# Attention over a pooled memory and experts on one core: sums as eight products, a maximum in pieces, another opening and smaller transfers

## The chip, the cores and the metric

The kernel runs on one core of one Trainium2 chip. The metric is the device time of one execution in microseconds, the median of several runs. The profile is one execution taken by the hardware profiler; its times are counted from the first instruction. PE is the tensor engine, DVE the vector engine, ACT the scalar engine, POOL GpSimd, SP the engine that issues nearly all transfers.

## The reference

There are 8 batches with 8 heads, 576 tokens and 64 values per head; phi holds 32 memory slots per head. Then comes a mixture of 8 experts (512 to 1024 to 512) over all 4608 tokens.

```python
a = np.exp(phi - np.max(phi, axis=2, keepdims=True))        # over the tokens
a = a / (np.sum(a, axis=2, keepdims=True) + 1e-09)
k_m = np.einsum('bhsm,bhsd->bhmd', a, k)
v_m = np.einsum('bhsm,bhsd->bhmd', a, v)
scores = np.matmul(q, k_m.transpose(0, 1, 3, 2)) / np.sqrt(64)
attn = softmax(scores)                                      # over the 32 slots
x = np.matmul(attn, v_m)                                    # heads joined: 512 per token
e_idx = argmax(x @ w_gate + modality_bias[modality_id])     # one expert per token
out = gate_w * (np.maximum(x @ w1[e_idx], 0) @ w2[e_idx])
```

## The kernel before, in words

**Layout.** The eight heads are two groups (NG) of four (HG): the groups lie on the two halves of the 128 partitions, 64 places of 9 tokens each. The memory of a batch is built first. `mem_max` (L309) takes the maximum of phi, by a `fold` (L291) of four DVE operations; `first_max` (L301) does it for batch 0 with reductions. `mem_exp` (L350) forms the exponentials, `mem_sums` (L374) adds them up on POOL, or on DVE for batch 0. `kv_products` (L392) multiplies them with keys and values in tiles of 64 x 32 (L403), and then adds over the partitions by one product of the sums with `sides` (L408), a matrix of ones and zeros that parts the two groups. `first_products`, `first_sums`, `first_divide`, `first_even`, `first_odd` (L410 to L477) are the steps of batch 0.

**Attention.** `q_turn` (L536) turns q in place on DVE. `scores` and `first_scores` (L541, L556) multiply; `soften` (L582) turns the scores to tokens, takes the maximum, subtracts it and has ACT form the exponential; `normalise` (L603) divides by the sum plus EPS and turns back. For batch 0's first part of four places, `first_weights` (L627) and `first_split` (L644) do it group by group. `a_split` (L652) splits the weights into a rounded upper half (ACT) and a remainder (DVE), in tiles xa (first part) and xb (second part), and for odd batches stores both to DRAM, where only a fallback reads them.

**Experts.** The expert that the bias alone prefers is guessed early (`guess`, L215) and its w1 and w2 are loaded; `verdict` at the end says whether a token chose another one, and only then does the fallback `any_experts` run. `value_products` (L724) multiply the pooled values with w1, so that `hidden` (L765) needs one product of attention weights with that matrix vw, in three terms (upper x upper, remainder x upper, upper x remainder). `relu` (L786) evicts on ACT (hh) and DVE (hl). `outputs` (L805) multiplies with w2 in three terms; `store` (L832) scales by the gate on ACT and issues the store on SP.

**The order.** All instructions are issued in an order that a planner works out before the build (`weave`, L1131): two lists, attention and experts, each with costs per engine (`TAKES`, L860), places in the progress of the expert work (`due`) and earliest times (`floor`). `weave` follows both lists and takes the next attention step when its due progress is reached and its inputs would be ready. An output product counts fully in the progress, a hidden one 0.35 (`WORTH`, L881). `HOLD` (L1138) says how much attention work may be queued on DVE in front of the eviction of the next hidden product. `AHEAD` and `EARLIER` (L1116) shift the memory steps of a batch: at L1123 the value of EARLIER is subtracted, so that {3: -4.0} puts batch 3 four units later. The opening, batch 0, is a list written out by hand in `plan_first` (L914).

**Idle products.** `warm_small` (L162) issues small products of zeros (64 x 32, 16 columns), `warm` (L156) large ones (128 x 128, 512 columns). `BUSY` (L79) has the counts before the opening; `nothing(n)` in `plan_first` (L945, L947, L989) puts n large ones between its steps.

**Transfers.** SP's queue has, in the opening: phi of batch 0, k, v, the first part of q; then, once the expert is guessed, w1 in two halves, modality ids and w_gate between them, w2, the rest of q, phi of batch 1 (L223 to L239); then k and v of batch 1 and q of batch 1 in 32 pieces (`more_keys`, L489). k and v of a batch are one transfer each (`load_kv`, L177).

## Time and profile before

| | |
|---|---|
| median of 3 runs | 389.59 us (389.57 to 389.6) |
| profiled execution | 389.69 us, of which 387.9 us is the span from first to last instruction |
| DVE, ACT, POOL busy | 244.7, 141.3, 45.8 us |
| mean granted clock of PE | 0.994 |
| moved by DMA | 56.89 MB, mean 147 GB/s |

The page lists busy times of the engines, the span in 40 slices, the DMA queues, the chain that ended last and the costliest groups of instructions. In a row of a timeline stand the start, the length, the engine with the line of the kernel, the operation, what it writes and reads, and the count of instructions that were merged; in square brackets is the idle time of the engine just before, and what ended it. A product of f32 operands shows as two records.

### The profile page before, as it was taken

To read this page: it belongs to the slowest core of one execution; us is meant where nothing else is said; L and a number is where in the kernel's file an instruction comes from. 1 tells how busy PE (TensorE), PEld (TensorE's weight loads), DVE (VectorE), ACT (ScalarE), POOL (GpSimd) and SP (SyncE) were. 2 spreads that over 40 slices of the span, in tenths; PEclk is the share of its full clock that TensorE was granted. 3 is DMA by queue.
4 is the path that set the end of the run, shared out by engine and by line. 5 is a ranking of instruction groups with operands and counts; after the bars stand their busy time and mean duration, and the time that the engine had idled before them with its cause. 6 is when DMAs were issued, how large, how long until landed. Compare 5 with 4: busy or idle time off the path is not lost.

```text
span 387.9 us, 9645 instructions
## 1 busy us (share of the span) xinstructions
PE 375.3 (97%) x3891; PEld 303.3 (78%) x3893; DVE 244.7 (63%) x613; ACT 141.3 (36%) x327; POOL 45.8 (12%) x116
## 2 busy tenths in 40 slices
PE   6899999999999999999999999999999999999993
PEld 3577976889779886788879887798868878698982
DVE  4787756895786389836786476864887467750400
ACT  2382524425234243433433334323443325241410
POOL 4347030023000400030000300003000200000000
PEclk9999999999999999999999999999999999999997
DMA  8998679875761397639712397614411011531111
GB/s 300 379 394 183 103 140 344 225 210 150 243 120 42 94 298 184 208 82 276 119 34 56 75 300 126 255 28 119 182 29 42 15 30 27 198 102 32 28 36 55
DMA packets 91307, 56.89 MB, mean 147 GB/s; under 512 B 69236, under 2 KB 74356, under 8 KB 91252
## 3 DMA queue, kind: packets, MB, share of 16 engines
q1 hardware_dynamic: 90976, 55.87, 51.4%
q8 instruction: 33, 0.54, 0.6%
q10 hardware_dynamic: 276, 0.30, 0.2%
q14 instruction: 22, 0.18, 0.2%
HBM read 37.28 MB, written 18.87 MB: 145 GB/s over the span
## 4 chain that ended last, share of the span: by engine, by line
PE 85%; DVE 4%; SPq 4%; DMA 3%; ACT 1%; issue 1%; ACTq 0%
PE pe L816 47%; PE pe L779 24%; PE pair L403 4%; PE pe L732 3%; DMA q_sb<-in_q_dram 3%; SPq L195 3%; PE pair L548 2%; PE pair L679 1%; SPq L178 1%; DVE vwl L154 1%; PE pair L148 1%; PE pair L732 1%; PE pair L408 1%; DVE xbl L662 0%; ACT ob L829 0%
## 5 line engine op out<-in xcount | busy, mean ns | idle before, releaser
L816 PE MATMUL pe<-w2h,hh 128*128 128x512 f32 x288 | 116.3, 404 | 0.0
L816 PE MATMUL pe<-w2h,hl 128*128 128x512 f32 x288 | 112.4, 390 | 0.0
L816 PE MATMUL pe<-w2l,hh 128*128 128x512 f32 x288 | 110.3, 391 | 0.0
L796 DVE SCALAR_TENSOR_TENSOR hl<-pe,hh 128x256 fp32r<-128x256 f32 (+2 forms) x158 | 58.3, 392 | 43.1 <-ACT hh L792 42.3
L816 PEld LDWEIGHTS pe<-w2h,hh 128*128 128x128 f32 x288 | 54.1, 188 | 19.8 <-issue 9.7
L792 ACT ACTIVATE hh<-pe 128x256 fp32r<-128x256 f32 (+2 forms) x158 | 53.4, 362 | 41.6 <-PE pe L779 41.2
L816 PEld LDWEIGHTS pe<-w2l,hh 128*128 128x128 f32 x288 | 54.0, 188 | 11.8
L816 PEld LDWEIGHTS pe<-w2h,hl 128*128 128x128 f32 x288 | 54.2, 188 | 9.6
L829 ACT ACTIVATE ob<-pe,gates 128x512 f32<-128x512 f32 x36 | 24.6, 687 | 73.4 <-PE pe L816 48.1
L779 PE MATMUL pe<-xbh,vwh 128*128 128x320 f32 x128 | 40.3, 315 | 0.1
L779 PE MATMUL pe<-xbh,vwl 128*128 128x320 f32 x128 | 39.6, 309 | 0.0
L779 PE MATMUL pe<-xbl,vwh 128*128 128x320 f32 x128 | 39.6, 309 | 0.0
L779 PE MATMUL pe<-xah,vwh 128*128 128x256 f32 x124 | 35.2, 287 | 1.5 <-DVE hl L796 0.7
L779 PE MATMUL pe<-xal,vwh 128*128 128x256 f32 x124 | 35.0, 284 | 0.3 <-DVE xal L662 0.3
L779 PE MATMUL pe<-xah,vwl 128*128 128x256 f32 x124 | 34.9, 283 | 0.0
L337 POOL COPY ts<-tm 32x4 f32<-32x4 f32 x24 | 4.8, 199 | 198.8 <-DVE tm L329 198.1
L779 PEld LDWEIGHTS pe<-xah,vwh 128*128 128x128 f32 x124 | 23.6, 191 | 4.2 <-ACT xah L648 1.6
L779 PEld LDWEIGHTS pe<-xbh,vwh 128*128 128x128 f32 x128 | 24.0, 188 | 1.7 <-issue 0.9
L779 PEld LDWEIGHTS pe<-xbl,vwh 128*128 128x128 f32 x128 | 24.1, 188 | 0.3
L779 PEld LDWEIGHTS pe<-xal,vwh 128*128 128x128 f32 x124 | 23.7, 191 | 0.8 <-DVE xal L662 0.5
L779 PEld LDWEIGHTS pe<-xbh,vwl 128*128 128x128 f32 x128 | 24.0, 188 | 0.0
L779 PEld LDWEIGHTS pe<-xah,vwl 128*128 128x128 f32 x124 | 23.7, 191 | 0.0
(173 smaller groups left out, 430.0 us busy)
## 6 DMA issues: line engine op xcount, KB each, us to landing
kv_sb<-in_k_dram SPq DMA_DIRECT2D x8, 1152.0 KB, 7.2
kv_sb<-in_v_dram SPq DMA_DIRECT2D x8, 1152.0 KB, 9.7
out_dram<-ob SPq DMA_DIRECT2D x64, 128.0 KB, 2.4
q_sb<-in_q_dram SPq DMA_DIRECT2D x112, 72.0 KB, 2.8
ph<-in_phi_dram SPq DMA_DIRECT2D x7, 576.0 KB, 4.3
raw<-in_moe_w_dram SPq DMA_DIRECT2D x2, 1024.0 KB, 6.4
raw<-in_moe_w_dram SPq DMA_DIRECT2D x1, 1280.0 KB, 10.2
out_dram<-ob SPq DMA_DIRECT2D x4, 256.0 KB, 2.1
```

The costliest lines, as they stand in the source:

```text
L148: nc.tensor.transpose(dst, src, ident[:rows, :rows])
L154: nc.vector.tensor_tensor(l, src, h.bitcast(F32), op=ALU.subtract)
L195: nc.sync.dma_start(*later.pop(0))
L337: nc.gpsimd.tensor_copy(ts_[BL * a:BL * (a + 1)], live["tm"][BL * o:BL * (o + 1)])
L403: nc.tensor.matmul(live["kvp"][M * j:M * (j + 1), g], lhsT=pe[half, j, c * M:(c + 1) * M], rhs=kv_sb[half, :, j, c * D:(c + 1) * D], start ...
L548: nc.tensor.matmul(sc[g][M * j:M * (j + 1), a, 0:QC * BL], lhsT=kvT[b][rows, 0, M * j:M * (j + 1)], rhs=qT[rows, j, a], start=True, stop=T ...
L732: nc.tensor.matmul(pvs[g][M * j:M * (j + 1), :], lhsT=vT[b][rows, j, :], rhs=raw1[rows, j, cols], start=True, stop=not more, tile_position ...
L779: nc.tensor.matmul(ph[:, 0:n], lhsT=(vl if k == 2 else vh)[:, g, cols], rhs=xl if k == 1 else xh, start=(g == k == 0), stop=(g == NG - 1 a ...
L792: nc.scalar.activation(hs[0][:, f, h0:h0 + p1 - p0], live["ph", f][:, p0:p1], AF.Relu)
L796: nc.vector.scalar_tensor_tensor(hl, live["ph", f][:, p0:p1], 0.0, hh.bitcast(F32), op0=ALU.max, op1=ALU.subtract)
L816: nc.tensor.matmul(po, lhsT=tile_columns(hl if n == 1 else hh, f, t), rhs=(w2l if n == 2 else w2h)[:, f, :], start=(f == n == 0), stop=(f ...
L829: nc.scalar.activation(ob, po, AF.Copy, scale=gate_of(b, t))
```

## The change

- **Idle products**: 97 small and 3 large ones ahead of the opening in place of 92 and 10; the 1, 4 and 3 large ones between its steps go.
- **Sums**: in `kv_products` the product with `sides` becomes eight products of 64 x 32 with a column of ones, one per head; `sides` and its fills go.
- **Maximum**: for batch 1 the fold goes; reductions take the maximum of heads 0 and 1 before the second scores of batch 0, of head 2 before batch 0's second normalisation, of head 3 before the remainder of its split.
- **EPS**: batch 0's first part keeps its weights in a tile with a 33rd column that holds EPS, so that the sum contains it and the addition goes.
- **Order of the opening**: `first_odd` for the keys stands ahead of the turns of q, `first_even` for the values ahead of `first_keys`; floors move by 0.5 to 1.
- **Planner**: `EARLIER` {3: -4.0} becomes {7: -6.0}; `HOLD` rises from 1.9, 2.4, 2.2 to 2.2, 3.0, 2.7; the cost of the key and value products falls from 2.6 to 2.5, and kinds "m1" (DVE 0.55) and "m2" (DVE 1.1) are added in `TAKES`.
- **Transfers**: w1 in four pieces of 256 columns; k and v of batches 1 to 7 in two pieces each, by columns; the stored operands with runs of one place (NG x 128 values) instead of all places of a partition. The fallback reads them accordingly.
- **Last tile**: the last store of the last batch is scaled half by ACT, half by DVE, and the halves are stored by the queues of SP and ACT.

```diff
@@ -76,7 +76,7 @@
     EPS = 1e-9
-    BUSY = 92, 10
+    BUSY = 97, 3
...
@@ -135,8 +134,8 @@
-    xa_dram = [[dram.tile([P, NG * RA * P], F32R, name=f"xa_dram{p}{x}") for x in "hl"] for p in range(NPAIR)]
-    xb_dram = [[dram.tile([P, NG * RB * P], F32R, name=f"xb_dram{p}{x}") for x in "hl"] for p in range(NPAIR)]
+    xa_dram = [[dram.tile([RA, P, NG * P], F32R, name=f"xa_dram{p}{x}") for x in "hl"] for p in range(NPAIR)]
+    xb_dram = [[dram.tile([RB, P, NG * P], F32R, name=f"xb_dram{p}{x}") for x in "hl"] for p in range(NPAIR)]
@@ -168,6 +167,9 @@
+    def flat(x, n):
+        return x.rearrange("p i g c x -> p (i g c x)").rearrange("p (n y) -> p n y", n=n)
+
@@ -175,7 +177,11 @@
-        nc.sync.dma_start(kv_sb[:, t], halves((k, v)[t], b))
+        src = halves((k, v)[t], b)
+        pieces = 2 if b else 1
+        for i in range(pieces):
+            cols = slice(i * (QC * D // pieces), (i + 1) * (QC * D // pieces))
+            nc.sync.dma_start(kv_sb[:, t, :, cols], src[:, :, cols])
@@ -219,8 +225,9 @@
         for hf in range(2):
-            cols = slice(hf * 512, (hf + 1) * 512)
-            nc.sync.dma_start(raw1[:, :, cols], first[:, :, cols])
+            for c0 in (2 * hf, 2 * hf + 1):
+                cols = slice(c0 * 256, (c0 + 1) * 256)
+                nc.sync.dma_start(raw1[:, :, cols], first[:, :, cols])
@@ -298,13 +305,16 @@
+    def heads_max(b, js):
+
+        if js.start == 0:
+            live["top", b] = wk.tile([P, HG, M], F32, name="top")
+        src = phs[b].rearrange("p j (c m) -> p j m c", m=M)
+        nc.vector.tensor_reduce(live["top", b][:, js], src[:, js], axis=AX.X, op=ALU.max)
+
     def first_max():
-
-        top = wk.tile([P, HG, M], F32, name="top")
-        src = phs[0].rearrange("p j (c m) -> p j m c", m=M)
         for js in (slice(0, HG // 2), slice(HG // 2, HG)):
-            nc.vector.tensor_reduce(top[:, js], src[:, js], axis=AX.X, op=ALU.max)
-        live["top", 0] = top
+            heads_max(0, js)
@@ -394,7 +404,7 @@
-        live["psum"] = pk[:, 0, 2 * D:2 * D + NG]
+        live["psum"] = pk[:, :, 2 * D]
@@ -405,7 +415,13 @@
-        nc.tensor.matmul(live["psum"], lhsT=sums.rearrange("p j m -> p (j m)"), rhs=sides, start=True, stop=True)
+        for j in range(HG):
+            for g in range(NG):
+                half = slice(QP * g, QP * (g + 1))
+                nc.tensor.matmul(
+                    pk[M * j:M * (j + 1), g, 2 * D:2 * D + 1], lhsT=sums[half, j], rhs=ones_c[half],
+                    start=True, stop=True, tile_position=(QP * g, M * j),
+                )
@@ -583,7 +599,9 @@
         if step in (None, 0) and groups in (None, 0):
-            live["a", b, part] = by_token(wk.tile([P, 2 * NG * RB * M], F32, name="a", bufs=2), n, M)
+            live["a", b, part] = live["a0"][:, :, :, :, 0:M] if b == part == 0 else by_token(
+                wk.tile([P, 2 * NG * RB * M], F32, name="a", bufs=2), n, M
+            )
@@ -591,7 +609,7 @@
-                        a[:, g].rearrange("p a c m -> p a (c m)"), sc[g][:, :, RA * part * BL:(RA * part + n) * BL]
+                        a[:, g] if b == part == 0 else a[:, g].rearrange("p a c m -> p a (c m)"), sc[g][:, :, RA * part * BL:(RA * part + n) * BL]
@@ -631,8 +649,8 @@
             sa, ra = (wk.tile([P, 2 * NG * RB], F32, name=y, bufs=2)[:, 0:n] for y in ("sa", "ra"))
-            nc.vector.tensor_reduce(sa, x, axis=AX.X, op=ALU.add)
-            nc.vector.tensor_scalar_add(sa, sa, EPS)
+            whole = live["a0"][:, g].rearrange("p a c m -> p (a c) m")
+            nc.vector.tensor_reduce(sa, whole, axis=AX.X, op=ALU.add)
@@ -663,7 +681,7 @@
-                nc.sync.dma_start(d.bitcast(F32), x.rearrange("p i g c x -> p (i g c x)").bitcast(F32))
+                nc.sync.dma_start(d.bitcast(F32).rearrange("n p x -> p n x"), flat(x, n).bitcast(F32))
@@ -831,6 +849,15 @@
         def finish(po):
+            if b == B - 1 and t is None:
+                rows = out[S * (b - 1):S * (b + 1)].rearrange("(p c) d -> c p d", c=QC)[QC - 1]
+                first, second = slice(0, DM // 2), slice(DM // 2, DM)
+                obs = [wk.tile([P, DM], F32, name="ob", bufs=2)[:, 0:DM // 2] for _ in range(2)]
+                nc.scalar.activation(obs[0], po[:, first], AF.Copy, scale=gate_of(b, t))
+                nc.vector.tensor_scalar(obs[1], po[:, second], gate_of(b, t), None, op0=ALU.mult)
+                nc.sync.dma_start(rows[:, first], obs[0])
+                nc.scalar.dma_start(rows[:, second], obs[1])
+                return
...
@@ -895,7 +922,7 @@
         for name, after, what, late in (
-            ("max", [], mem_max, 0.0),
+            *((("max", [], mem_max, 0.0),) if b > 1 else ()),
@@ -942,20 +969,18 @@
         add(("guess",), "guess", [], guess)
-        nothing(1)
         add(("exp", 0), "first exp", [("top", 0)], mem_exp, 0)
-        nothing(4)
...
         add(("kn", 0), "kn0", [("k", 0), ("sums", 0)], first_divide)
+        add(("ko", 0), "ko0", [("kn", 0)], first_odd, 0)
         turns(0, 0, 9.5)
-        add(("ko", 0), "ko0", [("kn", 0)], first_odd, 0)
...
         add(("v", 0), "v0", [("exp", 0)], first_products, 1)
+        add(("vn", 0), "vn0", [("v", 0)], first_even, 1)
         add(("kT", 0), "kT", [("ko", 0)], first_keys)
-        add(("vn", 0), "vn0", [("v", 0)], first_even, 1)
@@ -986,7 +1011,6 @@
-        nothing(3, "pe")
@@ -994,10 +1018,11 @@
         some_hidden("he", "h0y", [("x", 0, 0)], range(1, 3), range(1, 2))
-        add(("start",), "start", [], lambda: None, floor=25.0)
-        turns(1, 0, 26.5)
-        turns(1, 1, 27.2)
-        add(("s", 0, 1), "s1", [("qt", 0, 1, 1), ("vwl", 0, 1)], first_scores, RA, RB, floor=28.6)
+        add(("start",), "start", [], lambda: None, floor=24.0)
+        turns(1, 0, 25.5)
+        turns(1, 1, 26.2)
+        add(("max", 1, 0), "m2", [], heads_max, 1, slice(0, 2), floor=26.5)
+        add(("s", 0, 1), "s1", [("qt", 0, 1, 1), ("vwl", 0, 1)], first_scores, RA, RB, floor=27.6)
@@ -1049,6 +1074,11 @@
                 add(("bias", pair + 1), "nothing", [], biases, pair + 1)
+        if b == 0:
+            names = [x[0] for x in todo]
+            for j, before in ((3, ("x", 0, 1)), (2, ("n", 0, 1, 0))):
+                todo.insert(names.index(before), (("max", 1, j - 1), "m1", [], heads_max, (1, slice(j, j + 1))))
+            todo += [(("max", 1), "nothing", [("max", 1, 2)], lambda: None, ())]
@@ -1086,7 +1116,7 @@
-            stage(experts, ("w2", c), "w2", [], first_w2, c, floor=21.0 + 0.7 * c)
+            stage(experts, ("w2", c), "w2", [], first_w2, c, floor=20.5 + 0.7 * c)
@@ -1113,7 +1143,7 @@
-    AHEAD, EARLIER, SPREAD = (5.8, 5.0), {3: -4.0}, 0.55
+    AHEAD, EARLIER, SPREAD = (5.8, 5.0), {7: -6.0}, 0.55
@@ -1135,7 +1165,7 @@
-        HOLD = {"h0": 1.9, "h1": 2.4, "h3": 2.2}
+        HOLD = {"h0": 2.2, "h1": 3.0, "h3": 2.7}
@@ -1211,13 +1241,12 @@
         warm(BUSY[1])
+        live["a0"] = wk.tile([P, NG, 2, RA, M + 1], F32, name="a0")
+        nc.gpsimd.memset(live["a0"][:, :, :, :, M:M + 1], EPS)
...
         nc.scalar.activation(minus, ident, AF.Copy, scale=-1.0)
-        for g in range(NG):
-            for e in range(NG):
-                nc.gpsimd.memset(sides[QP * g:QP * (g + 1), e:e + 1], float(g == e))
...
```

More of the change, by code (lines that the diff above doesn't have):

```diff
@@ L103, in attn_moe @@
     places = const.tile([P, 2], F32, name="places")
-    sides = const.tile([P, NG], F32, name="sides")
     busy = const.tile([P, 512], BF16, name="busy")
@@ L864, in attn_moe @@
         "exp": (0.0, "T1.5 A0.7"), "exp0": (0.35, "D1.5 A0.7"), "first exp": (0.35, "D1.5 A0.7"), "first sums": (0.0, "T1.9"), "sums": (0.0, "P2.9"),
-        "vwp": (1.15, ""), "vwpu": (1.25, "A1.1"), "vwu": (0.0, "A1.15"), "vwl": (0.0, "D1.35"),
[1 row of a table removed]
[2 rows of a table added]
         "kT": (0.45, "A0.4"), "vT": (0.3, "A0.35"), "kvT": (0.45, "A0.4"),
@@ L1309, in any_experts @@
                 for x, d in zip(xa + live["xb"], xa_dram[pair] + xb_dram[pair]):
-                    nc.gpsimd.dma_start(x.rearrange("p i g c x -> p (i g c x)"), d)
+                    n = d.shape[0]
+                    nc.gpsimd.dma_start(flat(x, n), d.rearrange("n p x -> p n x"))
                 for i in range(2):
```

3 rows, old and new, of the table TAKES are left out of this document.

## The prediction

> **What bounds the kernel now.** I read the page first, then the waits of TensorE (PE), then the timeline of the first 45 us engine by engine, then the chain that ended last, then the tail.
>
> ```profile
> span 387.9 us, 9645 instructions
> PE 375.3 (97%) x3891; PEld 303.3 (78%) x3893; DVE 244.7 (63%) x613; ACT 141.3 (36%) x327; POOL 45.8 (12%) x116
> ```
>
> PE is busy for 97% of the span, and no other engine comes near. So the kernel is a stream of matrix products with a start, a few holes and a tail, and an edit can only win by shortening a product, closing a hole, or shortening start or tail. The holes of PE, by what ended them (total, times, longest):
>
> ```profile
> PE pair L148 <- DVE top L306: 1.1, 1, 1.1
> PE pe L779 <- DVE hl L796: 0.7, 1, 0.7
> PE pair L566 <- ACT kT L518: 0.5, 1, 0.5
> PE pe L779 <- ACT xah L659: 0.5, 1, 0.5
> PE pair L732 <- ACT kvT L523: 0.4, 1, 0.4
> PE pe L779 <- DVE xal L662: 0.3, 1, 0.3
> PE pair L148 <- DVE keys L466: 0.3, 1, 0.3
> PE pe L779 <- ACT xah L648: 0.3, 1, 0.3
> ```
>
> No DMA stands in this list, and nearly all of it lies in the opening; only the lines of L796, L659 and L662, 1.5 us together, lie behind it. The opening on PE, from the second of the large idle products on (start, length, engine and line):
>
> ```profile
> 3.12 0.63 PE L159 MATMUL pair<-busy 128*128 128x512 bf16 x1 [0.22 <-issue]
> ...
> 6.77 0.30 PE L148 MATMUL pair<-ident,top 128*128 128x128 f32 x1 [1.05 <-DVE top L306]
> 6.91 0.38 PE L159 MATMUL pair<-busy 128*128 128x512 bf16 x1
> 7.46 0.44 PE L361 MATMUL pe<-ident,topc 128*64 128x128 f32 x4 [0.17 <-DVE peak L212]
> 7.83 1.04 PE L159 MATMUL pair<-busy 128*128 128x512 bf16 x4
> 8.97 0.36 PE L251 MATMUL pair<-row,ones_r 1*128 1x17 f32 x2
> 9.26 2.19 PE L422 MATMUL pair<-kv_sb,exp 64*64 64x128 f32 x72
> 11.51 0.29 PE L433 MATMUL pair<-ones_c,sums 64*64 64x1 f32 x8
> 11.65 2.17 PE L422 MATMUL pe<-kv_sb,exp 64*64 64x128 f32 x72
> 14.15 0.43 PE L148 MATMUL pair<-ident,keys 128*128 128x128 f32 x2 [0.32 <-DVE keys L466]
> 15.04 1.07 PE L566 MATMUL pair<-q_sb,kT 32*32 32x128 f32 x64 [0.46 <-ACT kT L518]
> ```
>
> This is one chain through four engines: maximum, exponentials, products with keys (9.26) and values (11.65), the turned keys (14.15), the scores (15.04). After the scores DVE works off a softmax for two head groups, and PE last waits for the second of them:
>
> ```profile
> 22.02 0.82 PE L159 MATMUL pe<-busy 128*128 128x512 bf16 x2
> 23.09 0.38 PE L779 MATMUL pe<-xah,vwh 128*128 128x256 f32 x1 [0.26 <-ACT xah L648]
> ```
>
> From 23.09 us on PE runs dense. Whatever the opening saves counts if it moves this point; what it saves elsewhere does not.
>
> **The idle products.** Seven large ones go ahead of 6.77, where PE stands idle for 1.05 us waiting for DVE: worth nothing by themselves. The single one (6.91) is followed by a wait for DVE: nothing. The four (7.83) stand ahead of the key products, which could start up to 0.2 us sooner (9.26 less the end of the row vector's product, without the queue in front); but the products for the sums at 11.51 wait for DVE's sums, so the values start where they did: nothing. The last ones (22.02) stand in front of a wait and hide nothing but it: nothing. What they did besides is keep PE occupied; if that was needed, the price is the first rival's. Five more small ones are a few hundredths ahead of an idle PE.
>
> **Keys before the turns of q.**
>
> ```profile
> 12.74 0.71 DVE L539 STREAM_TRANSPOSE q_sb<-q_sb 128x512 f32<-128x512 f32 x1 [0.31 <-DMA q_sb<-in_q_dram]
> 13.38 0.82 DVE L466 SCALAR_TENSOR_TENSOR keys<-pair,recs,even 128x64 f32<-128x64 f32 x4
> ```
>
> The keys sat behind the first turn, which sat behind q's transfer; they now start up to 0.64 us sooner (13.38 - 12.74). But PE can turn them only after the value products (11.65 + 2.17 = 13.82), so at most 0.33 us before 14.15; ScalarE (ACT) now copies the even value halves ahead of the turned keys; and the scores need both turns of q, which end where they did, since DVE does the same three pieces in another order. Bounds 0 and 0.33; I take 0.1, near the lower end, because the second turn ends late either way.
>
> **The column of EPS.**
>
> ```profile
> 18.65 0.17 DVE L635 TENSOR_SCALAR sa<-sa 128x8 f32<-128x8 f32 x1
> ```
>
> ```profile
> 22.64 0.41 ACT L648 CAST xah<-aT 128x256 fp32r<-128x256 f32 x1 [0.44 <-DVE aT L642]
> ```
>
> Each head group loses one such addition, and both lie on DVE's chain towards the second copy at 22.64: 2 x 0.17 = 0.34 us. The sums read 33 elements in place of 32, about 0.01 us each; strided rows cost something between nothing and a tenth of six operations of this size (0.25). I take 0.35 for the additions and nothing for the stride. With the 0.1 above, the copy ends at 22.6 in place of 23.05, and the dense stream starts **0.45 us earlier** (bounds 0.1 and 0.7). The next thing late could be the weights:
>
> ```profile
> 9.10 0.39 SPq L223 DMA_DIRECT2D raw<-in_moe_w_dram  x1
> ```
>
> ```profile
> raw<-in_moe_w_dram SPq DMA_DIRECT2D x2, 1024.0 KB, 6.4
> ```
>
> The first half of w1 is on chip at about 9.10 + 6.4 = 15.5, and is read only after the scores (15.04 + 1.07). In quarters the same bytes move, with two more issues on SP's queue at 0.39 each ahead of w2, the rest of q and phi of batch 1; that is 0.8 us on loads that are limited by bytes. Nothing to 0.3 us; I take nothing. Later keys, values and the stored operands in smaller pieces make SP issue about 14 more transfers of half the size; no wait of PE names a DMA, so nothing, within 0.3 either way.
>
> **The maximum of batch 1 in pieces.** The fold of four operations leaves DVE's queue; four reductions of one head each come in, two alone and two together. The two together stand behind the later turns of q and in front of the softmax that waits for the second scores:
>
> ```profile
> 31.15 0.91 DVE L593 STREAM_TRANSPOSE a<-pair 128x320 f32<-128x320 f32 x2 [1.85 <-PE pair L566]
> ```
>
> DVE idles 1.85 us there, enough for two heads (the opening's own maximum of four heads ends the 1.05 us hole, so a head is below that). The other two stand in front of operations that wait for ACT. Cover exists, so nothing; should phi of batch 1 be late, everything behind on DVE is, by up to 1 us.
>
> **Eight products for the sums**, in batches 1 to 7 (chain that ended last: start, length, count):
>
> ```profile
> 171.66 2.18 PE pair L403 x144
> 173.84 0.31 PE pair L408 x2
> ```
>
> ```profile
> 192.10 0.19 PE pair L528 x8
> ```
>
> One product goes (two records, 0.31 us); eight small ones come (sixteen records). At the rate of the key and value products, 2.18/144 = 15 ns, they take 0.24; at that of L528, 0.19/8 = 24 ns with the switch of shape in it, 0.38. So between +0.07 and -0.07 per batch. I take 0.21 x 0.15 = 0.03 of gain, since they continue the pattern of the products before them, times seven: **0.2 us** (bounds -0.5 and 0.5).
>
> **The order planned anew.** Batch 3's memory steps move earlier by 4 of the planner's units, batch 7's later by 6, and attention work may queue on DVE up to 0.3 to 0.6 us deeper ahead of evictions (HOLD).
>
> ```profile
> 163.06 0.39 PE L779 MATMUL pe<-xah,vwh 128*128 128x256 f32 x1 [0.74 <-DVE hl L796]
> ```
>
> This hole is DVE's backlog: batch 3's gate, and right behind it the maximum of batch 4, all in front of the evictions of batch 3's hidden part. With batch 3 earlier, the gate is out of the way. Of the 0.74 I take 0.7. The two holes of batch 1 (0.5 and 0.3 in the list) lie on its own softmax, for which no due time changes; only its maximum has gone from the queue. Of 0.8 I take 0.2. For batch 7:
>
> ```profile
> 332.63 0.68 DVE L662 TENSOR_TENSOR xal<-aT,xah 128x512 fp32r<-128x512 f32 x1
> ```
>
> ```profile
> 341.06 5.75 PE pe L779 x48
> ```
>
> Its operands are ready 7.7 us before PE reads them; 6 units, about 6 us of output products, fit, barely. Sum **0.9 us** (bounds -1 and 1.5).
>
> **The last tile** is scaled by ACT and DVE, half each, and stored by two queues:
>
> ```profile
> 381.54 0.69 ACT L829 ACTIVATE ob<-pe,gates 128x512 f32<-128x512 f32 x1 [4.75 <-PE pe L816]
> ```
>
> Half a row on ACT took 0.41 (the copy at 22.64), so 0.28 less, and half the bytes per transfer: **0.3 us** (0.1 to 0.4). Nothing queues behind either.
>
> **Sum.** 0.45 + 0.2 + 0.9 + 0.3 = 1.85 us from the profiled execution's 389.69: 387.84. That execution stands 0.1 above the median of 389.59, so 387.7.
>
> **Rivals.**
> *The clock.* The first large product took 0.63 us, the one at 6.91 only 0.38: PE ran at half clock at first and at full clock once it had been occupied. At the end it falls back (third-last number: granted clock):
>
> ```profile
> 383.00:383.50 0.50, 0.00 (x0) 0.00 (x0) 0.00 (x0) 0.00 (x0) 0.00 (x0) 0.93 0.78 283
> 383.50:384.00 0.50, 0.00 (x0) 0.00 (x0) 0.00 (x0) 0.00 (x0) 0.00 (x0) 0.50 0.60 209
> ```
>
> The last product was out before 381.54, so about 2 us of idleness were enough. In the new opening the three large products are over by 3.12 + 2 x 0.63 = 4.4, and only short products come until 9.26. If the key products then run at half clock, they take 2.2 us more; the values end at 16.0, the keys turn 1.85 later, and with 0.45 back the opening loses 1.4: 389.69 + 1.4 - 1.4 (the other three terms) - 0.1 = **389.6**, no change. Against it: the pause contains real products, and I can't see what the clock counts. Chance 0.2. The Trainium skill, "TensorE: Matmul & The Clock Gate", section "The HAM clock gate", says that the full clock is granted after about 3.4 us of sustained activity and withdrawn after an idle window of that length. By it the shortened warm-up would be too short and the streams would lose half of one window, an estimate of 1.7 us, so about 389.1; the trace's withdrawal after some 2 us is sooner than its rule.
> *The clock through both streams*, keys and values: 2.19 + 2.17 lost, 0.33 + 0.45 saved, so 3.6; 389.59 + 3.6 - 1.4 = **391.8**, slower. It decides as soon as more than the key products run slow. Chance 0.07.
> *DVE's deeper queue.* A hole as at 163.06 may open in each hidden part of batches 2 to 7, twelve places, because the planner lets attention work in ahead of evictions. At 0.4 us in half of them, 2.4, without the 0.9 of the replanning: 389.59 - 0.95 + 2.4 = **391.0**, slower. It decides once a backlog outlasts the four banks that PE may fill ahead. For it: the one such hole is there already. Against it: evictions idle between pieces in all other places. Chance 0.15.
>
> **Numbers.** Forecast 0.58, clock low for the keys 0.2, for both 0.07, deeper queue 0.15. A measurement here can tell 0.2%, 0.8 us. The forecast's own range is 386.6 to 388.8; the range given reaches over the first rival to 390.3. Of these four, in this order, faster: 0.56 + 0.05 + 0 + 0.01 = 0.62; same: 0.02 + 0.14 + 0 + 0.05 = 0.21; slower: 0 + 0.01 + 0.07 + 0.09 = 0.17.
>
> **What would show it.** Right: the second group's first hidden product near 22.6; one hole fewer behind 100 us; a last ACT step of about 0.4; the sums' segment below 0.31. Wrong: key products of over 3 us, new waits of L779 on hl, or a product that waits for a transfer.

## The result, and the profile after

The changed kernel takes **391.7 us** in the median of 7 runs (390.52 to 393.31), the kernel before 389.6 us (389.35 to 390.19, 7 runs) on the same chip: a ratio of 1.0058, interval 1.0035 to 1.0081. It is slower by about 0.6%, 2.1 us, where 1.9 us of gain had been forecast. Two executions far above all others (418.53 us of the kernel before, 738.26 us of e15 below) count in no ratio. The profiled execution took 392.31 us, its span 390.5 against 387.9.

The page of the changed kernel first: PE is still the bound, busy for as long as before (375.3 us then), in a span that is 2.6 us longer. Since fifteen large idle products went and PE is busy for as long without them, other products must have become longer.

```profile
span 390.5 us, 9854 instructions
PE 375.7 (96%) x3981; PEld 303.7 (78%) x3981; DVE 245.1 (63%) x611; ACT 140.6 (36%) x327; POOL 45.5 (12%) x113
```

PE's waits in the changed kernel (total, times, longest):

```profile
PE pair L147 <- POOL mine L213: 3.4, 1, 3.4
PE pair L438 <- ACT exp L381: 0.6, 1, 0.6
PE pe L797 <- ACT xah L666: 0.6, 1, 0.6
PE pair L544 <- DVE a L611: 0.6, 1, 0.6
```

The wait ahead of the first turned maximum (L147, then L148) was 1.1 us and is 3.4, mostly because the seven large idle products that filled it are gone; the maximum also comes 0.45 us later (7.22 against 6.77). All three holes behind 60 us (0.5, 0.3 and 0.7 us) are gone; one of 0.6 at L544 is new. The timeline of the opening on PE shows where the rest is:

```profile
7.22 0.45 PE L147 MATMUL pair<-ident,top 128*128 128x128 f32 x1 [3.42 <-POOL mine L213]
8.05 0.70 PE L371 MATMUL pe<-ident,topc 128*64 128x128 f32 x4 [0.38 <-DVE peak L218]
8.75 0.57 PE L258 MATMUL pair<-row,ones_r 1*128 1x17 f32 x2
9.95 4.12 PE L438 MATMUL pair<-kv_sb,exp 64*64 64x128 f32 x72 [0.63 <-ACT exp L381]
13.84 0.34 PE L449 MATMUL pair<-ones_c,sums 64*64 64x1 f32 x8
14.02 3.09 PE L438 MATMUL pe<-kv_sb,exp 64*64 64x128 f32 x72
17.05 0.44 PE L147 MATMUL pair<-ident,keys 128*128 128x128 f32 x2
18.01 1.07 PE L582 MATMUL pair<-q_sb,kT 32*32 32x128 f32 x64 [0.53 <-ACT kT L534]
...
25.84 0.39 PE L797 MATMUL pe<-xah,vwh 128*128 128x256 f32 x1 [0.62 <-ACT xah L666]
```

Put beside the opening shown in the prediction: the key products start 0.69 us later (9.95 against 9.26) and last 4.12 us for the same 72 products (2.19); the values last 3.09 (2.17). The same instructions on the same operands in nearly twice the time: PE's clock was low, through the keys and into the values. The page's row of the granted clock doesn't show it, because it has no record ahead of the first rise; that rise stands in the trace's clock records at 15.93 us, and at 4.55 us in the kernel before. The scores start at 18.01, 2.97 us late, and the second group's first hidden product at 25.84, 2.75 late. From scores to that product it is 7.83 us, 8.05 before.

From there the stream to the last product's start takes 383.25 - 25.84 = 357.41 us; before, 381.06 - 23.09 = 357.97. So all parts of the change that act in the stream brought 0.56 us together. The last tile, in the timeline of the end:

```profile
383.25 0.39 PE L834 MATMUL pe<-w2l,hh 128*128 128x512 f32 x1
383.72 0.47 ACT L856 ACTIVATE ob<-pe,gates 128x256 f32<-128x256 f32 x1 [4.75 <-PE pe L834]
384.22 0.36 SPq L858 DMA_DIRECT2D out_dram<-ob  x1
384.23 0.48 DVE L857 TENSOR_SCALAR ob<-pe,gates 128x256 f32<-128x256 f32 x1 [15.76 <-ACT ob L856]
```

The two halves do not run side by side: DVE, idle for 15.76 us, starts when ACT is done. Together they take 0.99 us, where one ACT step took 0.69. From the last product's start to the end it is 7.25 us instead of 6.84. Not all of that need be the halves': in traces of kernels with the whole tile the same stretch is 6.54 (e2) to 7.44 us (e4). The account of the span is thus 2.75 - 0.56 + 0.41 = 2.6 us.

### The profile page after: what moved, and what is told of

Its sections match the earlier page's. It is cut to its first block, busy times and chain, and to the rows that moved or that the text cites. A ratio compares the mean times of both kernels' runs of the same rounds, so it can differ in the third digit from the quotient of the medians.

```text
span 390.5 us, 9854 instructions
## 1 busy us (share of the span) xinstructions
PE 375.7 (96%) x3981; PEld 303.7 (78%) x3981; DVE 245.1 (63%) x611; ACT 140.6 (36%) x327; POOL 45.5 (12%) x113
## 4 chain that ended last, share of the span: by engine, by line
PE 89%; DVE 3%; SPq 2%; DMA 2%; ACT 1%; issue 1%; ACTq 0%; POOL 0%; POOLq 0%
PE pe L834 50%; PE pe L797 26%; PE pe L750 3%; PE pair L413 3%; SPq L201 2%; PE pair L564 2%; PE pair L697 1%; DMA row<-n_moe_modality_bias_dram 1%; PE pair L438 1%; DMA out_dram<-ob 1%; PE pe L438 1%; PE pair L582 1%; PE pair L147 0%; PE pair L544 0%; DVE a L611 0%
## 5 line engine op out<-in xcount | busy, mean ns | idle before, releaser
L834 PE MATMUL pe<-w2h,hl 128*128 128x512 f32 x288 | 112.5, 391 | 0.0
L814 DVE SCALAR_TENSOR_TENSOR hl<-pe,hh 128x256 fp32r<-128x256 f32 (+2 forms) x158 | 57.5, 389 | 38.8 <-ACT hh L810 38.0
L797 PE MATMUL pe<-xbh,vwh 128*128 128x320 f32 x128 | 40.3, 315 | 0.0
L797 PE MATMUL pe<-xbh,vwl 128*128 128x320 f32 x128 | 39.5, 309 | 0.0
L797 PE MATMUL pe<-xbl,vwh 128*128 128x320 f32 x128 | 39.5, 309 | 0.0
L797 PE MATMUL pe<-xah,vwh 128*128 128x256 f32 x124 | 35.2, 287 | 0.6 <-ACT xah L666 0.6
L797 PE MATMUL pe<-xal,vwh 128*128 128x256 f32 x124 | 34.9, 283 | 0.0
L797 PE MATMUL pe<-xah,vwl 128*128 128x256 f32 x124 | 34.9, 283 | 0.0
L797 PEld LDWEIGHTS pe<-xah,vwh 128*128 128x128 f32 x124 | 23.6, 191 | 2.8 <-ACT xah L666 1.7
L152 ACT CAST vwh<-pe 128x512 fp32r<-128x512 f32 x26 | 14.0, 590 | 30.9 <-PE pe L750 30.9
L797 PEld LDWEIGHTS pe<-xbh,vwh 128*128 128x128 f32 x128 | 24.0, 188 | 1.2 <-DVE hl L814 0.6
L797 PEld LDWEIGHTS pe<-xbl,vwh 128*128 128x128 f32 x128 | 24.0, 188 | 0.3
L797 PEld LDWEIGHTS pe<-xbh,vwl 128*128 128x128 f32 x128 | 24.0, 188 | 0.1
L797 PEld LDWEIGHTS pe<-xal,vwh 128*128 128x128 f32 x124 | 23.7, 191 | 0.2
```

The costliest lines, as they stand in the source:

```text
L152: nc.scalar.copy(h, src)
L797: nc.tensor.matmul(ph[:, 0:n], lhsT=(vl if k == 2 else vh)[:, g, cols], rhs=xl if k == 1 else xh, start=(g == k == 0), stop=(g == NG - 1 a ...
L814: nc.vector.scalar_tensor_tensor(hl, live["ph", f][:, p0:p1], 0.0, hh.bitcast(F32), op0=ALU.max, op1=ALU.subtract)
L834: nc.tensor.matmul(po, lhsT=tile_columns(hl if n == 1 else hh, f, t), rhs=(w2l if n == 2 else w2h)[:, f, :], start=(f == n == 0), stop=(f ...
```

## The experiments

Theory at the start: the missing idle products cost some 2 us by the clock, and the rest of the change works about as forecast. Rival: the idle products cost nothing, and the loss comes from the new order, the transfers or the sums. None of these kernels leaves out part of the computation. "Hole" in the table means a pause of PE of over 0.2 us, from the key products on, that its list of waits puts down to "issue", to no engine and no transfer. The first of e1 and of e4, the last of e3 and the one in brackets are put down to an engine; they are counted because they stop at the same places of the program as others do (below). The holes are those of the profiled execution alone, which lies 1.0 to 1.5 us below the median in e1, e4, e5 and e14, and 2.2 above it in e12.

| kernel | median us | before, same chip | ratio, interval | holes |
|---|---|---|---|---|
| after | 391.7 | 389.6 | 1.0035 to 1.0081 | none |
| e1 after, idle products as before | 395.4 | 389.86 | 1.0121 to 1.0192 | 1.7, 1.5 |
| e2 before, idle products of after | 391.72 | 389.86 | 1.0033 to 1.006 | none |
| e3 after, two idle calls back | 396.1 | 389.86 | 1.0135 to 1.0187 | 2.0, 1.3, 1.4, 0.9 |
| e4 e1, last tile as before | 395.39 | 389.86 | 1.0127 to 1.0159 | 1.3, 1.5 |
| e5 e4, 82 small idle products | 391.74 | 390.0 | 1.0037 to 1.0077 | 0.3 |
| e6 before, 102 small idle products | 390.26 | 390.0 | 1.0001 to 1.0019 | none |
| e7 e5, transfers as before | 391.17 | 390.0 | 1.0023 to 1.0052 | 0.9, 1.3 |
| e8 e5, planner's constants as before | 395.65 | 390.0 | 1.0131 to 1.0172 | 0.6, 1.7, 0.6 |
| e9 e4, sums as one product | 389.93 | 390.03 | 0.9985 to 1.0014 | none |
| e10 before, eight sums | 393.79 | 390.03 | 1.0062 to 1.0129 | 1.35, 1.5 |
| e11 e9, transfers as before | 389.44 | 390.03 | 0.9971 to 0.999 | none |
| e12 e10, 62 small idle products | 391.41 | 389.97 | 1.0025 to 1.0053 | 0.3, 1.2 |
| e13 e11 with eight sums, 72 small | 389.51 | 389.97 | 0.9976 to 0.9995 | 0.5 (0.8) |
| e14 as e13, 52 small | 391.39 | 389.97 | 1.0019 to 1.0046 | 0.3, 0.9 |
| e15 as e13, 32 small | 394.21 | 389.97 | 1.0095 to 1.0143 | 0.5, 1.1, 1.1, 1.5 |
| e16 as e13, 62 small | 389.68 | 390.03 | 0.9983 to 1.0 | 0.2 |
| e17 e10, 75 small | 391.12 | 390.03 | 1.0021 to 1.0046 | 0.4, 1.4, 0.7 |

### The clock: e1 to e3

e1 gives the changed kernel its idle products back; e2 takes them from the kernel before; e3 restores only the two calls ahead of the key products.

```diff
-    BUSY = 97, 3
+    BUSY = 92, 10
...
         add(("guess",), "guess", [], guess)
+        nothing(1)
         add(("exp", 0), "first exp", [("top", 0)], mem_exp, 0)
+        nothing(4)
...
+        nothing(3, "pe")
         add(("xu", 0, 0, 1), "xu1", [("n", 0, 0, 1, 1)], first_split, 1, 0)
```

> The changed kernel with the idle products of before put back (92 small and 10 large ahead, 1, 4 and 3 between the steps). If the half clock made the loss, the key products take 2.2 us again instead of 4.1, the first product of the second head group starts near 22.8 us instead of 25.8, and the time is about 389.2 with a spread of a few tenths. If the order, the smaller transfers or the tail made it, the time stays at 391 to 392.

> The kernel before with only its idle products cut as in the change (97 small, 3 large, none between the steps). If the half clock made the loss: key products of 3 to 4.4 us, time 391.5 to 392.6 with a spread of 2 us or more between runs. If another part of the change made it: 389.6 as before.

> The changed kernel with only the 1 and the 4 large products back between its steps; 97 small and 3 large ahead stay. If only the pause right ahead of the key products matters: about 389.3. If the clock must have been raised before by the 10 large ones: 390.5 to 392, as the changed kernel.

e2 bears the clock out: 1.9 us slower (ratio 1.0047) by this edit alone. Its opening on PE:

```profile
6.76 0.45 PE L148 MATMUL pair<-ident,top 128*128 128x128 f32 x1 [2.97 <-POOL mine L207]
...
9.50 3.69 PE L422 MATMUL pair<-kv_sb,exp 64*64 64x128 f32 x72 [0.63 <-ACT exp L371]
13.02 0.23 PE L433 MATMUL pair<-ones_c,sums 64*64 64x1 f32 x8
13.11 2.16 PE L422 MATMUL pe<-kv_sb,exp 64*64 64x128 f32 x72
```

The keys take 3.69 us, the values 2.16: here the clock rose at 12.62 us, at the end of the keys, and in the changed kernel only within the values. The spread of 2 us or more that was expected did not come (390.98 to 392.03). e3 decides nothing: its keys are slow too (3.24 us from 10.81 on), but its 396.1 us lies outside both of its expectations, because of holes. e1's key products are back at 2.2 us. Yet e1 is 3.7 us slower than the changed kernel, and not 2 faster: the theory's second half fell. The key, value and sum products of a batch follow each other closely and are called its run here. At the end of batch 4's run e1's timeline of PE shows:

```profile
173.73 1.96 PE L413 MATMUL pair<-kv_sb,exp 64*32 64x128 f32 x121
175.43 0.26 PE L421 MATMUL pair<-ones_c,sums 64*32 64x1 f32 x12
177.21 0.23 PE L421 MATMUL pair<-ones_c,sums 64*32 64x1 f32 x4 [1.51 <-issue]
```

In the middle of the sixteen records of the eight sum products PE stops for 1.51 us and waits for nothing the profile knows. Another stands at 93.3, behind batch 1's sums; e3 has four. The changed kernel as submitted has none.

### Holes that no wait explains: e4 to e8

e4 undoes the last tile as well; e5 takes ten small idle products away; e6 adds ten in the kernel before; e7 and e8 undo the transfers or the planner's constants in e5.

```diff
-            if b == B - 1 and t is None:
...
-                return
```

```diff
-    BUSY = 92, 10
+    BUSY = 82, 10
```

e6 has 102 there. e7, e8:

```diff
-            for c0 in (2 * hf, 2 * hf + 1):
-                cols = slice(c0 * 256, (c0 + 1) * 256)
+            for c0 in (hf,):
+                cols = slice(c0 * 512, (c0 + 1) * 512)
...
-        pieces = 2 if b else 1
+        pieces = 1
```

```diff
-    AHEAD, EARLIER, SPREAD = (5.8, 5.0), {7: -6.0}, 0.55
+    AHEAD, EARLIER, SPREAD = (5.8, 5.0), {3: -4.0}, 0.55
...
-        HOLD = {"h0": 2.2, "h1": 3.0, "h3": 2.7}
+        HOLD = {"h0": 1.9, "h1": 2.4, "h3": 2.2}
```

> As e1_after_idle, and the last tile scaled by ACT alone and stored by one transfer, as before. In the changed kernel the two halves ran one after the other (0.47 + 0.48 us, against 0.69 for the whole tile). If that order is forced, this is 0.25 to 0.4 us faster than e1_after_idle. If two engines and two queues help in spite of it, it is 0.1 to 0.3 slower than e1_after_idle.

> As e4_idle_tail with 82 small idle products in place of 92, so that as many products stand ahead of the dense stream as in the changed kernel. Theory of the blocks: PE's program arrives in blocks of 16 KB, and ten products more or less shift the place where a block ends against the dense runs of small products; then the holes of 1.4 to 2 us that end without a releaser go, and the time falls from 395 to about 388.9. Theory of the idle products as such (the large ones harm, whatever their place): stays at 394 to 395. Ten small products by themselves are 0.1 us.

> The kernel before with 102 small idle products in place of 92, nothing else. By the theory of the blocks the shift alone can open one to three holes of 1 to 2 us: 390.5 to 394. If the holes come from the new order or the smaller transfers: 389.6 to 389.8 as before.

> As e5_idle82_tail, with w1 in halves, keys and values whole and the stored operands in long runs, as before. If the smaller transfers cost nothing and gain nothing: within 0.2 of e5_idle82_tail. If they keep the program's blocks from waiting behind long transfers: slower by 0.5 to 2, with holes that have no releaser. If they hinder: faster by 0.3 or more.

> As e5_idle82_tail, with EARLIER and HOLD as before. The prediction put 0.9 us on the new order, 0.7 of it on the hole in front of batch 3's hidden part. If that is right: slower by about 0.7 than e5_idle82_tail, with a hole of 0.7 in front of a product of L797 near 160 us. If the new order is worth nothing: the same within 0.2.

e4 equals e1: the last tile is worth nothing that can be measured, though 0.3 us could hide in intervals this wide. e5 is 3.65 us faster than e4 in the medians (3.1 in the profiled executions), by ten products of zeros fewer in a stretch where PE waits anyway; the 388.9 us expected did not come. Batch 4's run is whole again (timeline of PE):

```profile
171.62 2.25 PE L413 MATMUL pair<-kv_sb,exp 64*32 64x128 f32 x144
173.60 0.29 PE L421 MATMUL pair<-ones_c,sums 64*32 64x1 f32 x16
173.83 0.50 PE L834 MATMUL pe<-w2h,hh 128*128 128x512 f32 x1
```

What the number of idle products changes, besides their time, is the place of everything behind them in PE's program. The DMA view of each hole shows one packet of a queue called "instruction", 16 KB, just ahead; every hole ended 1.2 to 1.6 us after that packet did. Counted in PE's records (products and weight loads), the holes of all runs stop at nearly the same numbers, whatever work stands there: about 442, 695, 1455, 2466, 3219, 4236, 5999 and 7010. These are steps of (7010 - 442) / 26 = 252.6 records. Counted with PE's semaphore instructions, some 110 that the traces hold beside these records, the holes stop at 448 or 449, 704 to 706, 1471, 2496 to 2498, 3263, 4288 or 4289, 6079 and 7103: each within two of 448 plus a multiple of 256. So I formed a second theory: PE's program comes in pieces of that length, and where PE runs through a piece of small products faster than the next arrives, it stops. The place between two pieces is called a cut below. The Trainium skill, "Runtime: NRT & Kernel Launch", section "Instruction fetch mechanics", has blocks of 16 KB and 256 instructions, which agrees; that crossing one is "mostly hidden" holds for most of the some 30 crossings of each trace, and not for these holes. e6 fits neither of its expectations: ten more idle products open no hole in the kernel before, and cost 0.26 us. e7 (where the stored operands are whole again too) and e8 do not isolate what they undo, since their holes differ as well; e8 also waits 2.1 us for ACT at 60.6 us. e8 does show the planner's part of the hole at 163 us: with the old constants it is back, in the timeline of PE,

```profile
168.41 0.39 PE L797 MATMUL pe<-xah,vwh 128*128 128x256 f32 x1 [0.75 <-DVE hl L814]
```

### The sums: e9 to e11

A batch's 144 key-value products make 288 records, with one sum product 292, with eight 320. e9 is e4 with the single product and `sides` back; e10 is the kernel before with the eight products and nothing else; e11 is e9 with the larger transfers.

```diff
-        nc.tensor.matmul(live["psum"], lhsT=sums.rearrange("p j m -> p (j m)"), rhs=sides, start=True, stop=True)
+        for j in range(HG):
+            for g in range(NG):
...
```

> The changed kernel with the before kernel's four calls of idle products and its single last tile (both as in the run at 395.4 us), and with the sums again as one product with the block of ones instead of eight small ones. Theory of the program blocks (the sums' eight small products, right behind the 128 small key-value products, lengthen the dense run in which PE uses up its program faster than the next 16 KB block comes, and move every later block boundary by 63 or so places): the holes of 1.3 to 2 us at batches 1 and 4 go or shrink, and the time is 387 to 391 us. Rival (the holes come from the planner's new order, whatever the sums): the holes stay and the time is 394 to 396 us.

> The kernel before with one part alone: the sums as eight small products instead of one. Prediction on record: 0.2 us faster, bounds plus and minus 0.5, so 389.1 to 390.1 us. Theory of the program blocks: the product itself saves 0.5 us or so, but the block boundaries lie elsewhere, and each that falls behind a dense run costs 1 to 2 us: 389 to 394 us, with at least one hole of over 1 us that no wait explains if it is over 390.5.

> The changed kernel with idle products, last tile, sums and transfers all as before; left of the change are the planner's order, the EPS column, the maximum in pieces and the reordered opening. Prediction on record for these parts: minus 1.35 us (0.45 in the opening, 0.9 from the planner), so 388.3 us. Rival (program blocks): the order of the work alone moves dense runs against the block boundaries, and a hole of 1 to 2 us or two take the gain back: 389.5 to 393 us.

e9 is 5.5 us faster than e4 by this one edit, and has no hole. e10 is 3.8 us slower than before by it; in the profiled executions 2.8 of that lies in the stream, which has the two holes, 0.7 in the opening and 0.3 in the tail. Its timeline of PE at batches 1 and 4:

```profile
93.08 2.25 PE L402 MATMUL pair<-kv_sb,exp 64*32 64x128 f32 x144
95.07 0.20 PE L410 MATMUL pair<-ones_c,sums 64*32 64x1 f32 x5
96.68 0.25 PE L410 MATMUL pair<-ones_c,sums 64*32 64x1 f32 x11 [1.35 <-issue]
...
176.17 0.23 PE L410 MATMUL pair<-ones_c,sums 64*32 64x1 f32 x9
177.90 0.24 PE L410 MATMUL pair<-ones_c,sums 64*32 64x1 f32 x7 [1.47 <-issue]
```

The DMA queues of the same kernel from 93.7 to 95.3 us hold the packet (packets, MB, share); from 95.3 to 97 there is none of this queue:

```profile
q8 instruction: 1, 0.02, 5.7%
q1 hardware_dynamic: 7, 0.01, 1.7%
```

The packet landed at 95.24 us, and PE went on 1.4 us later, at 96.68. The run of the same batch with one sum product, in e9's timeline of PE at batch 1:

```profile
87.07 2.33 PE L414 MATMUL pair<-kv_sb,exp 64*32 64x128 f32 x144
89.32 0.38 PE L419 MATMUL pair<-sides,sums 128*128 128x2 f32 x2
89.57 0.39 PE L792 MATMUL pe<-xbh,vwh 128*128 128x320 f32 x1
```

e11 holds what is left of the change beside transfers, sums, tail and idle products: 0.59 us faster than before (ratio 0.9981), about the bound of what can be told, where 1.35 had been forecast for these parts. Both expectations about it failed: no hole came, and the gain is less than half. It is the best version found, with e13 (0.9986) next to it; no other beats the kernel before by as much.

### Moving the cuts on purpose: e12 to e17

e12 and e17 are e10 with 62 and 75 small idle products, e13 to e16 are e11 with the eight sums and 72, 52, 32 and 62.

```diff
-    BUSY = 92, 10
+    BUSY = 62, 10
```

> The kernel before with the sums as eight products (as in the run at 393.8 us), and 62 small idle products in place of 92, so that all of PE's program after them stands 30 products earlier and the cuts between blocks fall 30 products later in the work. Theory (the cuts): the two holes of 1.35 and 1.47 us at the sums of batches 1 and 4 go or change their size, and the time moves by over 1 us, likely down to 390 to 392 us. Rival (the eight products themselves stall, wherever the cuts are): the holes stay at the sums' line with 1.3 to 1.5 us each and the time stays at 393 to 394.5 us.

> The run at 389.44 us (idle products, last tile and transfers as before; the new order, EPS column and maximum in pieces) with the eight sums back and 72 small idle products, not 92. Theory (the cuts): the time depends on the cuts alone: 388.5 to 389.3 us with no hole, 1 to 2 us more for each hole. The same kernel with 82 took 391.17 with holes of 0.9 and 1.3 us in the opening, so by that sum about 389.0 without them. Rival (the eight products cost time anywhere): 391 us or more at each of the three counts.

> As the run with 72 small idle products, with 52. Theory (the cuts): the opening's holes move or go again; 388.5 to 389.3 us without any hole, 1 to 2 us more for each. Rival (the eight products cost time anywhere): 391 us or more. A second rival, for this one: with so few small products the clock is granted late and the key products take over 3 us instead of 2.2, for some 2 us more.

> As the run with 72 small idle products, with 32. Theory (the cuts): 388.5 to 389.3 us without any hole, 1 to 2 us more for each. Rival (the eight products cost time anywhere): 391 us or more. A second rival: with so few small products PE idles before the opening, the clock is granted late, and the key products take over 3 us, for some 2 us more.

> The changed order with eight sums, and idle products, last tile and transfers as before (389.51 us with 72 small idle products, with holes of 0.5 and 0.8 us in the opening), now with 62. Theory (the cuts lie at about every 253rd record of PE; a hole comes where one falls 290 to 320 records behind the start of a batch's key-value products): no batch has a hole, the opening's come to some 0.3 to 0.7 us together, and the time is 388.7 to 389.4 us. Rival (the number of idle products matters for another reason, such as the clock): no better than with 72, or holes at batches.

> The kernel before with the eight sums alone (393.79 us with 92 small idle products and holes at batches 1 and 4; 391.41 with 62 and a hole at batch 7), now with 75. Theory (the cuts): by the count of records no batch has a cut 290 to 320 records behind the start of its key-value products, so no hole of over 0.6 us that no wait explains behind 50 us, and 389.2 to 390.4 us. Rival: a hole of over 1 us stays at the sums of some batch, and the time is over 390.8 us.

In e12 both holes are gone, and one has come at batch 7, where a cut now falls 305 records behind the run's start. An opposite case is the piece that ends in batch 7's run in e14, at number 7104: PE went through it in 1.75 us, faster than through any piece with a hole, and did not stop, for the next packet had landed 2.6 us before. e12's timeline of PE:

```profile
313.54 0.23 PE L410 MATMUL pair<-ones_c,sums 64*32 64x1 f32 x9
314.99 0.24 PE L410 MATMUL pair<-ones_c,sums 64*32 64x1 f32 x7 [1.20 <-issue]
```

e15 has three such holes, all at the sums (PE's waits):

```profile
PE pair L421 <- issue: 3.8, 3, 1.5
```

The key products took 2.19 to 2.20 us in the profiled executions of e14 and e15, so their second rival, the clock, falls for these two. It does not fall for e14's median, since its profiled execution, 389.91 us, is 1.5 us faster than that. In e12's profiled execution they took 3.82 us (from 11.12 on), and that execution is 2.2 us above the median of its runs (393.61 against 391.41): with 62 small products the clock was not safe in the order of before. With the eight sums, most holes in batches 1 to 7 stand 293 to 319 records behind a run's start, within its 320, and a few soon behind its end, where other cuts cost nothing (12 behind batch 4's run in the changed kernel); nor do cuts earlier in a run. By that count I foretold for e16 and e17 that no batch has a cut there. Neither has a hole within a batch's run. But e17 has one of 0.7 us soon behind batch 1's run (record 2467), and one in the opening that I had not reckoned with (timeline of PE):

```profile
20.91 0.72 PE L751 MATMUL pe<-vwh,minus 128*128 128x512 f32 x2 [1.40 <-issue]
```

That is record 696, on the count. So the cuts' places were right and my list of the stretches that suffer was too short; e17's 391.12 lies above the range expected. e16 came out 0.3 above its range, without a hole to blame. The traces also say what the eight sums save where no cut meets them. From the second group's first hidden product to the last product's start it is 357.72 us in e11, with one sum product, and 356.26 and 356.67 in e13 and e16, with eight. This gain of 1.0 to 1.5 us is lost again in their openings, where that hidden product starts at 23.99 and 24.09 instead of 22.98; so e13 equals e11, and e16 is no faster. Both refute the rival that eight sums cost time anywhere (391 us or more).

## Why the prediction was wrong, point by point

**The idle products were costed at nothing: this step failed.** "What they did besides is keep PE occupied" was named, and left to a rival. Alone, in e2, their going cost 1.9 us, because the clock stayed low and the key products took 3.69 us in place of 2.19. In the changed kernel the opening is 2.75 us late: 0.69 ahead of the keys, 1.68 in them, 0.6 at the end of the values, less 0.22 given back later. Of the 0.69, the 0.45 of the late maximum is not theirs: e2 has it at 6.76. The first rival had the keys' size right (2.2 us forecast, 1.93 more in the row), the second the extent, since the values ran slow too in the profiled execution; the 391.8 of the second is nearly the measured 391.7, though partly by chance: it counted 1.4 us of gains behind the opening, and the stream brought 0.56 and the tail lost 0.41. The two got a chance of 0.27 together. The argument against them, that the pause holds real products, was weak by rows that were there: without the large products the wait of 1.05 us ahead of the turned maximum grows to over 3, and about 2 us of idleness had ended the full clock in the tail. That 2 us was the low end, though: from PE's last product to the fall of the clock it is 1.98 (before) to 5.24 us (e4) over all the traces.

**Keys before the turns of q**: taken 0.1; in e11, with the clock at full, the scores start at 14.91 against 15.04, so 0.13, as forecast. One pair of executions does not bear out a tenth, though: from the first key product to the scores it is 5.5 us in e11 and also in e6, which has the order of before, 5.8 before and 6.3 in e10.

**The column of EPS**: taken 0.35. e11's second copy, in ACT's timeline:

```profile
22.52 0.40 ACT L661 CAST xah<-aT 128x256 fp32r<-128x256 f32 x1 [0.24 <-DVE aT L655]
```

Against 22.64 this is 0.12 sooner, as much as the scores. Between the two copies it saves 0.2 (20.11 to 22.52; before 20.03 to 22.64), but the first copy is 0.2 later after the scores. Nothing is left in e11, 0.2 in the changed kernel. What delays the first copy was not isolated.

**The sums**: taken 0.2 with bounds of 0.5 either way, that is 0.03 per batch. The timelines of PE have batch 4's run, in the changed kernel and then before, as

```profile
173.02 2.25 PE L413 MATMUL pair<-kv_sb,exp 64*32 64x128 f32 x144
175.01 0.29 PE L421 MATMUL pair<-ones_c,sums 64*32 64x1 f32 x16
175.24 0.50 PE L834 MATMUL pe<-w2h,hh 128*128 128x512 f32 x1
```

```profile
171.59 2.25 PE L403 MATMUL pair<-kv_sb,exp 64*32 64x128 f32 x144
173.77 0.38 PE L408 MATMUL pair<-sides,sums 128*128 128x2 f32 x2
174.02 0.48 PE L816 MATMUL pe<-w2h,hh 128*128 128x512 f32 x1
```

To the next output product it is 2.22 us instead of 2.43, and nearly the same in every batch, so seven batches save some 1.4 us: the term was too small, and its upper bound too low. The lower bound failed too: a run that is 28 records longer lets a cut fall inside it, at 0.9 to 1.7 us each, and e10 measures 3.8 us of loss where at most 0.5 was allowed. No row of the kernel before shows such a hole, and none of its runs has a cut in its last 50 records. In the changed kernel as submitted the last cut in a run lies 88 records ahead of its end; its loss is the clock's.

**The planner's order**: taken 0.9. The hole at 163.06 went, as forecast (0.7), and came back with the old constants in e8. Batch 1's holes went too, more than forecast, but L544, with batch 1's gate, now waits 0.6 us. Behind 60 us, 1.5 us of holes closed. Only 0.25 arrives in the stream of e11's profiled execution (357.72 against 357.97), because the output products themselves became dearer, in groups of e11:

```profile
L829 PE MATMUL pe<-w2h,hh 128*128 128x512 f32 x288 | 117.0, 406 | 0.0
L829 PE MATMUL pe<-w2h,hl 128*128 128x512 f32 x288 | 112.6, 391 | 0.0
L829 PE MATMUL pe<-w2l,hh 128*128 128x512 f32 x288 | 110.6, 392 | 0.0
```

340.2 us together, before 116.3 + 112.4 + 110.3 = 339.0. The planner's constants make this: e8, which has the old ones, needs 116.4 + 112.5 + 110.4 = 339.3 us, e5 without that edit 340.6. The new order changes between output products and others more often (117 times behind the opening, 103 before, 105 in e8); that this is the reason was not tried alone.

**Smaller transfers**: taken at nothing, within 0.3. The medians of e7 and e11, with the larger ones, are 0.6 and 0.5 us below those of e5 and e9, but the intervals overlap, e5's and e7's holes differ, and the stream takes the same time in e9 and e11 (357.68 and 357.72). So a cost of the smaller ones is not shown.

**The last tile**: taken 0.3 of gain. No gain could be told (e4 equals e1). The halves ran one after the other, 0.47 and then 0.48 us, where side by side had been assumed.

**The deeper queue of DVE** (third rival) did not come: no wait of L797 on hl over 0.2 us in the changed kernel.

## What to carry to other kernels

Products of zeros ahead of a stream are not idle: price them by the stream's own length at both clocks, and ask how long PE will stand still without them. A run of small products that has about as many instructions as one piece of PE's program (256 here) can be stopped by the program's own loading; look for waits put down to "issue" right behind an instruction packet, and compare versions at several numbers of idle products ahead before judging an edit of a microsecond.

## What the runs showed of the hardware that was not expected

- PE stopped for 0.2 to 2.0 us at some of the cuts between pieces of 256 instructions, mostly where dense small products led up to one, and went on 1.2 to 1.6 us after a 16 KB instruction packet had landed; ten small products fewer ahead moved the median of a kernel by 3.65 us (e4, e5).
- With 3 large idle products instead of 10 the 72 key products took 3.69 us (e2) or 4.12 (changed kernel) in place of 2.19, and the changed kernel's runs spread over 2.8 us (390.52 to 393.31), those of before over 0.8. The stretches at full clock last 372.05, 375.47, 378.88, 382.29 or 385.71 us in all traces, in steps of 3.41. The Trainium skill, "TensorE: Matmul & The Clock Gate", section "The HAM clock gate", has a window of 3.4 us that runs free of the kernel's start, which agrees with these steps and would give such a spread; by its 3.4 us of activity the keys, which start 8.6 us after the first idle products, should have been fast if the sparse opening counted as activity, so it did not.
- ACT and DVE did not read two halves of one output tile at the same time: DVE's half began 0.04 us after ACT's end. In the trace DVE's instruction waits for a semaphore that ACT's half sets, so this order is built into the program; whether the chip would allow both at once was not tried.
